# Output chains of the last head group one period later, and the queue engine's branch hint at the start of its stream

## The chip, the cores and the metric

The kernel runs on one core of one Trainium2 chip. The metric is the device time of one execution in microseconds (us). The profile's span is some 1.8 us shorter than that time (977.66 against 975.9 for the profiled run of the kernel before). Names of engines in the profile: PE is TensorE (matmuls), PEld its weight loads, ACT is ScalarE, DVE is VectorE, POOL is GpSimd, SP is SyncE, which issues nearly all DMA here.

## The reference

One sequence of 2048 rows and 1024 columns goes through two branches, and a gate per row mixes them:

```python
g = sigmoid((x * gate_w).sum(-1, keepdims=True))
a = A_ref(x, ...)            # a diagonal state-space layer: h = Lam_bar*h + Bu[t]; y = 2*Re(C h) + x*Dskip
b = B_ref(x, wqkv, wo)       # attention, 32 heads of 32 columns, then the output projection wo
return g * a + (1 - g) * b
```

What matters is the attention: 32 heads x 2048 x 2048 scores each need an exponential, and the output rows need the attention of all head groups before the projection `wo`.

## The kernel before

The program is planned in Python, in 512 periods. In period `p` PE computes the scores of one burst (4 heads, 256 queries, 256 keys), ScalarE takes two exponentials of 128x1024 from them, and PE multiplies the probabilities of burst `p - 2` with V. What PE has left in the period goes to blocks of four "dense" matmuls: projections, the state-space layer and, at the end, the output projection. Eight bursts make a unit (256 queries of one head group); there are 8 head groups of 8 units.

```python
def normalize(self, U):          # after the last burst of unit U: p % 8 == 1
    ...
    self.dma(lambda e: e.dma_start_transpose(self.OT[:, g, 256 * qb:256 * (qb + 1)]..., On[:, U % 2]...),
             [("On", U % 2)], [("OT", g, qb)] + x, "xp_o")

def d_out(self, qb, r, cb, k, js, kind):      # a chain: 8 matmuls = 2 periods; j is the head group
    for j in js:
        mms.append((1, lambda e, f, l, j=j: e.matmul(ps[:, 7, :], OT[:, j, ...], wo[j]..., start=f, stop=l),
                    [("OT", j, qb), wo[j][1]]))

# build(): when each output chain may start
seq = [(442, 6, r, cb, "part") for r, cb in rcb] + [(450, 7, r, cb, "part") for r, cb in rcb]
for qb in range(6):
    seq += [(458 + 8 * qb, qb, r, cb, "full") for r, cb in rcb]      # <- changed
seq += [(508, 6, r, cb, "rest") for r, cb in rcb]                    # one matmul each
```

The last matmul of a "full" chain (`j = 7`) reads the transpose that the last head group's unit has just started. After the last exponential comes a tail: the last probability-value matmuls, normalization, two PE transposes, four output matmuls, evacuation, two stores of 256 KB.

The fast path assumes that no softmax sum is out of range and checks this at the end. Every engine then reads a flag and branches over a slow fallback program. A hint in the instruction stream, placed by `MARK_AT`, is tied to that branch; what its place is worth is measured below (e2 and e6):

```python
MARK_AT = dict(pe=100, act=260, dve=260, pool=9999, sp=200)          # <- changed; counted back from the end
def stream(name, e):
    S.emit(name, e, sems, MARK_AT[name], lambda: loc.append(e.mark_branch_hint_location()))
    ...
    if name == "sp": S.final_waits(e, sems, False)                   # all DMAs but the last two
    e.wait_ge(sems[fast.flag_op.lane], fast.flag_op.tick)
    ... e.reg_load(r, flag[0:1, 0:1]); br = e.br_cmp(r, 0, on_true="done_" + name, ...); br.branch_hint(loc[0])
    ... # fallback program (cut)
    if name == "sp": S.final_waits(e, sems, True)                    # the last two stores
```

Of the kernel before, what the change touches and what calls it, by code (L numbers as in the profile page):

```python
# [937 lines left out]
class FastPath:  # L938
# [554 lines left out]
    def build(self):  # L1493
# [39 lines left out]
        rcb = [(r, cb) for r in range(2) for cb in range(2)]  # L1533
        seq = [(442, 6, r, cb, "part") for r, cb in rcb] + [(450, 7, r, cb, "part") for r, cb in rcb]
        for qb in range(6):
            seq += [(458 + 8 * qb, qb, r, cb, "full") for r, cb in rcb]
        seq += [(508, 6, r, cb, "rest") for r, cb in rcb]
        self.a_order = [4 * qb + 2 * r + cb for _, qb, r, cb, kind in seq if kind != "rest"]
        js = dict(full=range(8), part=range(7), rest=[7])
# [173 lines left out]
def bass_gated_mix__ssm_conv_s5__mha_block__prompt_kernel(  # L1713
    nc: bass.Bass,
    A_x: bass.AP,
    A_Lambda_re: bass.AP,
    A_Lambda_im: bass.AP,
    A_B_re: bass.AP,
    A_B_im: bass.AP,
    A_C_re: bass.AP,  # L1720
    A_C_im: bass.AP,
    A_log_dt: bass.AP,
    A_Dskip: bass.AP,
    B_x: bass.AP,
    B_wqkv: bass.AP,
    B_wo: bass.AP,
    gate_w: bass.AP,
    out: bass.AP,
):
    d = dict(A_x=A_x, A_Lambda_re=A_Lambda_re, A_Lambda_im=A_Lambda_im, A_B_re=A_B_re, A_B_im=A_B_im,  # L1730
             A_C_re=A_C_re, A_C_im=A_C_im, A_log_dt=A_log_dt, A_Dskip=A_Dskip, B_wqkv=B_wqkv, B_wo=B_wo,
             gate_w=gate_w, out=out)
    MARK_AT = dict(pe=100, act=260, dve=260, pool=9999, sp=200)
    with ExitStack() as es:
        S = Sched(n_dma_lanes=14)
        S2 = Sched(n_dma_lanes=12, pool_in_order=True, serial_xpose=True)
        sems = {l: es.enter_context(nc.semaphore("f_" + l)) for l in S.lanes()}
        sems2 = {l: es.enter_context(nc.semaphore("g_" + l)) for l in S2.lanes()}
        go = es.enter_context(nc.semaphore("go"))
        flag = es.enter_context(nc.sbuf_tensor("flag", [1, 1], I32))  # L1740
        with ExitStack() as fs:
            fast = FastPath(nc, S, fs, d, flag)
            fast.build()
            S.prepare()
        with ExitStack() as gs:
            c = gp_setup(nc, S2, gs, d)
            c.PA = GpPhaseA(c)
            c.items_done = 0
            gp_phase_c(c, gs)
            S2.barrier()  # L1750
            c.PA.finish(c.items_done)
            S2.prepare()
        block = es.enter_context(nc.Block())

        def stream(name, e):

            loc = []
            S.emit(name, e, sems, MARK_AT[name], lambda: loc.append(e.mark_branch_hint_location()))
            if not loc:
                loc.append(e.mark_branch_hint_location())  # L1760
            if name == "pool":
                for _ in range(272):
                    e.nop()
            if name == "sp":
                S.final_waits(e, sems, False)
            e.wait_ge(sems[fast.flag_op.lane], fast.flag_op.tick)
            with e.register("bad_" + name) as r:
                e.reg_load(r, flag[0:1, 0:1])
                br = e.br_cmp(r, 0, on_true="done_" + name, on_false="bad_" + name, comp_op="IS_EQ")
                br.branch_hint(loc[0])  # L1770
                with e.bass.body("bad_" + name):
                    if name == "sp":
                        S.final_waits(e, sems, True)
                        e.nop().then_inc(go, 1)
                    e.wait_ge(go, 1)
                    S2.emit(name, e, sems2)
                    if name == "sp":
                        S2.final_waits(e, sems2)
                    e.br("done_" + name)
                e.bass.switch_bb("done_" + name)  # L1780
            if name == "sp":
                S.final_waits(e, sems, True)

        @block.sync
        def _(e):
            stream("sp", e)

        @block.tensor
        def _(e):
            stream("pe", e)  # L1790

        @block.vector
        def _(e):
            stream("dve", e)

        @block.scalar
        def _(e):
            stream("act", e)

        @block.gpsimd  # L1800
        def _(e):
            stream("pool", e)
# [28 lines left out]
```

## Time and profile before

Runs of the kernel before: 979.44, 977.06, 979.46 and 977.79 us, median 978.62.

The first lines are from the page of the kernel before: span, busy time by engine, ACT's busy tenths in 40 slices, the granted clock of PE in tenths, and the costliest group (count, then busy us and mean ns, then idle time before it and its releaser).

```profile
span 975.9 us, 33479 instructions
...
PE 905.2 (93%) x15207; PEld 488.4 (50%) x15432; DVE 522.6 (54%) x1206; ACT 944.8 (97%) x1034; POOL 8.4 (1%) x46
...
ACT  4789999999999999999999999999999999999997
...
PEclk9999999999999999999999999999999999999998
...
L1454 ACT ACTIVATE f_pt<-f_ps 128x1024 bf16<-128x1024 f32 x1024 | 940.8, 1258 | 14.2 <-PE f_ps L1448 14.0
```

ScalarE is the limit: its exponentials fill the span. One exponential is 1258 ns in the table but they follow each other every 0.92 us, because the records of neighbours overlap. The idle column counts from the end of a record to the start of the next: at 886 us, after a record of 1.325, stands there 0.188 us.

The chain of waits of the kernel before, in order of time (start us, length us, what), around one place where ScalarE is not the limit:

```profile
880.57 0.74 PE f_ps L1401 x4
881.31 4.09 DMA f_OT<-f_On
885.40 0.05 issue
885.45 0.39 PE f_ps L1401
885.84 0.36 PE f_ps L1448 x8
886.22 3.82 ACT f_pt L1454 x4
```

The output matmul (L1401) waits for the DMA transpose, the scores (L1448) stand behind it in PE's order, and the exponential waits for the scores. The same pattern is at 940.32 us. The waits of the kernel before, 870 to 950 us (us in total, times, longest), show both occurrences, on PE and on the weight load:

```profile
PEld f_ps L1401 <- DMA f_OT<-f_On: 2.0, 2, 1.0
...
PE f_ps L1401 <- DMA f_OT<-f_On: 1.1, 2, 0.6
...
ACT f_pt L1454 <- PE f_ps L1448: 0.2, 1, 0.2
```

Busy time by engine in windows of 3.41 us near the end of the kernel before; the third number from the right is PE's granted clock:

```profile
core 0: us, PE busy (x) PEld busy (x) DVE busy (x) ACT busy (x) POOL busy (x), PEclk, DMA share, GB/s
952.69:956.11 3.42, 3.17 (x55) 1.55 (x53) 1.23 (x5) 3.42 (x4) 0.00 (x0) 1.00 0.00 0
956.11:959.52 3.41, 1.56 (x46) 0.93 (x43) 0.25 (x1) 3.41 (x5) 0.00 (x0) 1.00 0.32 101
959.52:962.94 3.42, 2.32 (x49) 1.32 (x50) 1.06 (x2) 3.42 (x5) 0.00 (x0) 0.50 0.00 0
962.94:966.35 3.41, 2.76 (x59) 1.58 (x54) 1.24 (x3) 3.41 (x5) 0.00 (x0) 0.50 0.21 77
966.35:969.76 3.41, 2.15 (x36) 1.32 (x33) 3.24 (x19) 1.54 (x4) 0.00 (x0) 1.00 0.22 79
```

After the last full output chain PE has little to do (46% busy from 956.11 us), and the clock falls to half for 6.83 us. It is back before the last exponential ends at 967.34 us. The tail from there to the end of the span is 8.60 us. The windows are aligned to the clock's changes in this trace.

### The profile page before, as it was taken

Reading aid. Unit: us, or ns where it says so; the run is one execution under the profiler, and the core shown is the slowest. Engines: PE = TensorE matmul, PEld = TensorE weight load, DVE = VectorE, ACT = ScalarE, POOL = GpSimd, SP = SyncE. Lnnn points to the kernel's source line nnn. Section 1 sums busy time; section 2 is a strip of 40 time slices with the busy share of each in tenths; the row PEclk is TensorE's granted clock in tenths of the full one; section 3 lists DMA queues with packets and bytes.
Section 4 is the critical chain, followed back from the end, with each engine's and each line's share of the span. In section 5 each row is a group of like instructions: output and inputs, shape, how many; then the busy total and the mean of one; then the engine's idle time right before and its main releaser. Section 6 shows DMA issues by size and latency. Waiting matters only on the chain.

```text
span 975.9 us, 33479 instructions
## 1 busy us (share of the span) xinstructions
PE 905.2 (93%) x15207; PEld 488.4 (50%) x15432; DVE 522.6 (54%) x1206; ACT 944.8 (97%) x1034; POOL 8.4 (1%) x46
## 2 busy tenths in 40 slices
PE   8889999999999999999999999999999999899995
PEld 5644554554444464444644644444554446444443
DVE  4897789877778854511257711177765112232223
ACT  4789999999999999999999999999999999999997
POOL 2000000000000000000000000000000000000000
PEclk9999999999999999999999999999999999999998
DMA  9992302311135202130022201142101213133311
GB/s 209 177 149 44 45 21 50 65 24 40 40 70 97 57 5 44 36 80 29 8 48 59 53 26 40 40 91 51 40 5 40 94 37 104 51 91 108 111 58 61
DMA packets 157011, 60.89 MB, mean 62 GB/s; under 512 B 145600, under 2 KB 145600, under 8 KB 156864
## 3 DMA queue, kind: packets, MB, share of 16 engines
q1 hardware_dynamic: 153664, 57.89, 26.6%
q8 instruction: 122, 2.00, 0.9%
q10 hardware_dynamic: 3200, 0.80, 0.4%
q14 instruction: 25, 0.20, 0.1%
HBM read 16.79 MB, written 12.58 MB: 30 GB/s over the span
## 4 chain that ended last, share of the span: by engine, by line
ACT 89%; DVE 5%; PE 4%; DMA 1%; issue 0%; DVEq 0%
ACT f_pt L1454 89%; DMA f_OT<-f_On 1%; DVE f_OT L1218 1%; DVE f_OT L1214 1%; PE f_ps L1313 1%; PE f_ps L1448 1%; PE f_ps L1069 1%; PE f_ps L1470 1%; DVE f_OT L1216 1%; DVE f_OT L1215 0%; PE f_ps L1401 0%; PE f_ps L1295 0%; DVE f_V L1319 0%; PE f_ps L1081 0%; PE f_ps L1344 0%
## 5 line engine op out<-in xcount | busy, mean ns | idle before, releaser
L1454 ACT ACTIVATE f_pt<-f_ps 128x1024 bf16<-128x1024 f32 x1024 | 940.8, 1258 | 14.2 <-PE f_ps L1448 14.0
L1470 PEld LDWEIGHTS f_ps<-f_V,f_pt 128*128 128x128 bf16 x8192 | 239.0, 96 | 109.9 <-issue 105.9
L1470 PE MATMUL f_ps<-f_V,f_pt 128*128 128x33 bf16 x8192 | 291.4, 178 | 0.5 <-DVE f_On L1484 0.5
L1448 PE MATMUL f_ps<-f_Q,f_K 32*128 32x256 bf16 x4096 | 204.7, 274 | 26.1 <-ACT f_pt L1454 7.7
L1448 PEld LDWEIGHTS f_ps<-f_Q,f_K 32*128 32x128 bf16 x4096 | 60.9, 92 | 242.4 <-ACT f_pt L1454 233.8
L1344 PE MATMUL f_ps<-f_xT,f_wb 128*128 128x512 bf16 x448 | 117.2, 377 | 13.8 <-DVE f_Q L1302 2.6
L1295 PE MATMUL f_ps<-f_xT,f_wb 128*128 128x512 bf16 x434 | 113.6, 379 | 9.2 <-issue 2.1
L1383 DVE TENSOR_SCALAR f_Ag<-f_ps,f_gcol 128x512 f32<-128x512 f32 x32 | 24.0, 751 | 139.8 <-PE f_ps L1368 139.8
L1244 DVE TENSOR_TENSOR_SCAN f_ht<-f_pf,f_init,f_ut 128x512 bf16<-128x512 f32 x64 | 80.4, 1273 | 0.0
L1368 PE MATMUL f_ps<-f_cT_im,f_hp 128*128 128x512 bf16 x192 | 72.6, 378 | 6.0 <-DVE f_Ag L1383 2.9
L1348 DVE CAST f_ub<-f_ps 128x512 bf16<-128x512 f32 x64 | 44.2, 691 | 51.9 <-PE f_ps L1344 51.8
L1313 PE MATMUL f_ps<-f_wb,f_xT 128*128 128x128 bf16 x1024 | 67.0, 219 | 0.0
L1401 PE MATMUL f_ps<-f_wb,f_OT 128*128 128x512 bf16 x218 | 58.5, 380 | 5.2 <-DVE f_xT L1407 1.7
L1344 PEld LDWEIGHTS f_ps<-f_xT,f_wb 128*128 128x128 bf16 x512 | 40.4, 96 | 36.2 <-issue 4.5
L1313 PEld LDWEIGHTS f_ps<-f_wb,f_xT 128*128 128x128 bf16 x1024 | 57.6, 97 | 0.4 <-issue 0.2
L1295 PEld LDWEIGHTS f_ps<-f_xT,f_wb 128*128 128x128 bf16 x496 | 39.3, 96 | 34.8 <-DMA f_xT<-in_A_x_dram 1.0
L1407 DVE SCALAR_TENSOR_TENSOR f_xT<-f_ps,f_gcol,f_hp 128x512 bf16<-128x512 f32 (+1 forms) x28 | 21.0, 751 | 64.3 <-PE f_ps L1401 64.3
L1368 PE MATMUL f_ps<-f_cT_re,f_hp 128*128 128x512 bf16 x144 | 54.4, 378 | 0.0
L1302 DVE CAST f_Q<-f_ps 128x512 bf16<-128x512 f32 x31 | 21.4, 691 | 51.3 <-PE f_ps L1295 51.3
L1235 DVE TENSOR_TENSOR f_tq<-f_ub,f_Et 128x512 bf16<-128x512 bf16 x128 | 46.3, 419 | 0.1
L1235 DVE TENSOR_TENSOR f_tq<-f_ht,f_Et 128x512 bf16<-128x512 bf16 x128 | 46.3, 417 | 0.0
L1319 DVE CAST f_V<-f_ps 128x512 bf16<-128x512 f32 x32 | 22.2, 693 | 42.0 <-PE f_ps L1313 42.0
(114 smaller groups left out, 428.4 us busy)
## 6 DMA issues: line engine op xcount, KB each, us to landing
ag_scratch<-f_Ag SPq DMA_DIRECT2D x32, 256.0 KB, 2.0
f_hp<-ag_scratch SPq DMA_DIRECT2D x32, 256.0 KB, 2.8
f_wb<-in_B_wqkv_dram SPq DMA_DIRECT2D x21, 256.0 KB, 4.4
out_dram<-f_xT SPq DMA_DIRECT2D x16, 256.0 KB, 2.3
f_wb<-in_B_wo_dram SPq DMA_DIRECT2D x1, 1024.0 KB
f_OT<-f_On SPq DMA_TRANSPOSE x63, 2.4
f_wb<-in_B_wqkv_dram ACTq DMA_DIRECT2D x3, 256.0 KB, 3.9
f_wb<-in_B_wo_dram SPq DMA_DIRECT2D x1, 768.0 KB, 4.6
```

The costliest lines, as they stand in the source:

```text
L1235: ops.append((c, lambda: dve(lambda e: e.tensor_tensor(o, a, b, op), r, w)))
L1244: ops.append((1.25, lambda ri=ri: dve(lambda e: e.tensor_tensor_scan(ht[:, ri, :], rr, ut[:, ri, :], self.init[:, ri, j:j + 1], ALU.mult, ...
L1295: mms.append((1, lambda e, f, l, a=a: e.matmul(ps[:, bank, :], w[:, g % 2, part, a, :], xT[:, a, 512 * ch:512 * (ch + 1)], start=f, stop=l ...
L1313: m = e.matmul(ps[:, bank, 128 * q:128 * (q + 1)], xT[:, a, 128 * kt:128 * (kt + 1)], w[:, g % 2, 2, a, :], start=(a == 0), stop=(a == 7))
L1344: mms.append((1, lambda e, f, l, a=a: e.matmul(ps[:, 7, :], bT[:, n % 2, ri, a, :], xT[:, a, 512 * ch:512 * (ch + 1)], start=f, stop=l), [ ...
L1348: self.dve(lambda e: e.tensor_copy(self.ub[:, n % 2, ri, :], ps[:, 7, :]), [("bank", 7)], [("ub", n % 2, ri)], "evac_u")
L1368: mms.append((1, lambda e, f, l, j=j, ri=ri: e.matmul(ps[:, 7, :], hp[:, ri, j, cols], cT[ri][:, j, 512 * cb:512 * (cb + 1)], start=f, sto ...
L1383: self.dve(lambda e: e.tensor_scalar(a, ps[:, 7, :], self.gcol[:, 0, tt:tt + 1], None, ALU.mult), [("bank", 7), "g0"], [at], "evac_c")
L1401: mms.append((1, lambda e, f, l, j=j: e.matmul(ps[:, 7, :], OT[:, j, 256 * qb + 128 * r:256 * qb + 128 * (r + 1)], wo[j][0][:, 512 * cb:51 ...
L1448: m = e.matmul(ps[:, 2 * sl[h // 2] + h % 2, 256 * kl:256 * (kl + 1)], K[32 * h:32 * h + 32, g % 2, 128 * kt:128 * (kt + 1)], Q[32 * h:32 ...
L1454: self.act(lambda e, s=s, p=p: e.activation(pt[:, p], ps[:, 2 * s:2 * s + 2, :], ACT.Exp, scale=SCALE), [("S", s)], [("pt", p)], "exp")
L1470: m = e.matmul(ps[:, 6, o:o + 33], pt[:, p, h2, 256 * kl + 128 * qt:256 * kl + 128 * (qt + 1)], V[:, g % 2, 2 * i + kl, h, :], start=(i == ...
```

## The change

The intent of the first part: a full chain starts one period (some 1.83 us) later, so that the transpose has arrived when its last matmul is due. The intent of the second: SyncE's hint should come early enough to have an effect, so it goes to the start of its stream.

```diff
-            seq += [(458 + 8 * qb, qb, r, cb, "full") for r, cb in rcb]
+            seq += [(459 + 8 * qb, qb, r, cb, "full") for r, cb in rcb]
@@
-    MARK_AT = dict(pe=100, act=260, dve=260, pool=9999, sp=200)
+    MARK_AT = dict(pe=100, act=260, dve=260, pool=9999, sp=900)
```

The order of the built instructions shows what it does on each engine: on PE the chains' blocks shift by one period, on SyncE the hint moves from behind the first transposed outputs to the front, and VectorE, ScalarE and GpSimd are unchanged.

## The prediction

> **What bounds the kernel now.** ScalarE. The page's first table gives ACT 944.8 of 975.9 us (97%), and the chain that ended last is 89% ACT, nearly all one line: 1024 exponentials of 128x1024, 1258 ns busy each but issued every 0.92 us (944 us for 1024). Idle before them is 14.2 us in all, in 15 pieces, most of it before 154 us. The stages by windows show ACT at 100% from 200 us to the tail except 0.19 us lost in 870 to 890 and 0.14 in 930 to 950. After the last exponential (967.35 us) follows a tail of 8.6 us.

> **First part: the output chains of full rows one period (1.83 us) later.** Nothing is added or removed: the same blocks of four matmuls on PE, the same DVE and ACT order. The last of the eight matmuls of a unit's first chain needs the transposed output of head group 7. In the timeline and the chain of waits this transpose is issued at 881.31 and 940.32 us and the matmul starts only 4.1 us later, after 0.55 us of PE waiting each. Because PE runs in order, the next scores come late, and ACT loses 0.19 and 0.14 us there. One period more is three times that wait, so both should go: about 0.33 us on the critical path.

> Side effect: the full chains end one period nearer the four "rest" chains, so one nearly matmul-free period (957 to 959 us) is left instead of two. The windows show PE's granted clock at 0.5 from 959.5 to 966.3 us, right after that lull. [...] It may now vanish or move. While ACT bounds, it is free; in the tail it is worth about 0.3 us either way.

> **Second part: SyncE's branch hint first in its stream instead of at 150.4 us.** It costs 62 ns, now before the first input load: start about 0.1 us later. [...] The trace agrees for GpSimd: from its branch at 970.88 to the next instruction 2.5 us, against 0.4 us on ACT. SyncE's branch (973.15) is followed by a wait that ends at 975.45, with the last store's last completion at 975.43 us: the landing ends last, a fetch stall would hide behind it. So the hint gives nothing, unless fetches delay the store (3.9 us against a median of 2.3): up to 0.5 us.

> **Sum.** -0.33 +0.1 -0.2 (hint, doubtful): -0.4 us, 0.04%, below the 2.4 us between the runs before (mean with the profiled one 978.4).

> Predicted: 978.2 us, range 975.8 to 980.6. Faster by over 2%: 0.01; within 2%: 0.98; slower: 0.01.

> **What would show it right.** No wait of the output matmuls for the output transpose after 870 us; ACT unbroken from 154 us to the tail; about 944.8 us of ACT. Half clock starting later or gone. SyncE's last wait still ending with the store's last completion.

> **What would make it wrong.** [...]SyncE stalls over 2 us past the landing; a delay of the first loads is larger than 62 ns; the tail falls in the half-clock stretch; a wider spread between runs.

The sum: it came to -0.33 + 0.1 - 0.2 = -0.43, given as -0.4 us. For GpSimd the 2.5 and 0.4 us are measured.

## The result, and the profile after

The changed kernel took 978.65, 979.8, 978.8 and 978.71 us, median 978.75, against 978.62 before. The ratio is 1.0006 with a 95% interval of 0.9988 to 1.0023: the same. Here and below a ratio is the mean time of one kernel's fast runs over that of the other's of the same rounds, so it is not quite the ratio of the quoted medians.

The page of the changed kernel:

```profile
span 976.9 us, 33704 instructions
...
PE 935.0 (96%) x15432; PEld 487.9 (50%) x15432; DVE 522.9 (54%) x1206; ACT 944.7 (97%) x1034; POOL 8.4 (1%) x46
```

PE's 935.0 against 905.2 us is no effect. The trace of the kernel before lacks 225 matmul records (15207 against 15432), and the program has the same matmuls. The chain of waits of the changed kernel, 930 to 950 us, is one unbroken piece:

```profile
929.30 21.08 ACT f_pt L1454 x23
```

These are all the waits that the same view lists for the changed kernel from 870 to 950 us. The lines of output matmuls waiting for the DMA are gone, and ScalarE waits for nothing:

```profile
DVE f_xT L1407 <- PE f_ps L1401: 61.8, 22, 5.0
PEld f_ps L1448 <- ACT f_pt L1454: 23.4, 44, 0.6
PEld f_ps L1470 <- issue: 9.3, 44, 0.2
DVE f_rc L1483 <- PE f_ps L1470: 1.1, 5, 0.2
```

So the first part did what it should. The windows near the end of the changed kernel, with the columns as before, show what happened beside it:

```profile
952.99:956.40 3.41, 3.33 (x56) 1.71 (x56) 1.39 (x4) 3.41 (x6) 0.00 (x0) 1.00 0.09 19
956.40:959.82 3.42, 2.41 (x51) 1.19 (x49) 0.75 (x1) 3.42 (x5) 0.00 (x0) 1.00 0.23 79
959.82:963.23 3.41, 2.00 (x50) 1.22 (x50) 1.50 (x2) 3.41 (x5) 0.00 (x0) 1.00 0.01 3
963.23:966.64 3.41, 2.81 (x45) 1.48 (x44) 1.55 (x4) 3.41 (x4) 0.00 (x0) 0.50 0.20 77
966.64:970.06 3.42, 2.62 (x23) 1.19 (x21) 2.60 (x18) 0.79 (x3) 0.00 (x0) 0.50 0.23 81
```

The half clock began later and stayed until the end. The last exponential now ended at 966.88 us, 0.46 us earlier than before, but the tail took 10.05 instead of 8.60 us.

The tool for everything that follows is a division of the span into pieces, from the start times of the 1024 exponentials, the issue of the last store and its last completion. "First" is the start of the first exponential; "70 to 870" the time between the starts of these two; "last store issued" counts from the end of the last exponential; "landed" from that issue to the last of its 16 completions. The tail is the sum of the last two and what remains to the end (0.5 to 1.0 us). All times are us, each from one profile.

| run | first | 0 to 70 | 70 to 870 | 870 to end of last | last store issued | landed | tail | span |
|---|---|---|---|---|---|---|---|---|
| before | 12.76 | 78.49 | 733.87 | 142.23 | +4.25 | 3.84 | 8.60 | 975.94 |
| as changed | 12.93 | 78.50 | 733.87 | 141.58 | +5.79 | 3.75 | 10.05 | 976.93 |
| e1 chains only | 14.09 | 78.49 | 733.88 | 141.58 | +5.79 | 3.68 | 9.97 | 978.01 |
| e2 hint only | 13.53 | 79.66 | 733.87 | 141.74 | +4.57 | 3.92 | 8.99 | 977.80 |
| e3 chains, PE filled | 13.09 | 79.64 | 733.87 | 141.58 | +3.91 | 3.92 | 8.34 | 976.52 |
| e4 before, PE filled | 13.41 | 78.48 | 733.88 | 141.72 | +3.91 | 3.86 | 8.28 | 975.77 |
| e5 filled, no branch | 13.15 | 80.76 | 733.88 | 141.58 | +3.91 | 2.11 | 6.50 | 975.88 |
| e6 hint late | 12.88 | 79.69 | 733.87 | 141.58 | +4.62 | 4.12 | 9.71 | 977.73 |
| e7 before, 506 filled | 13.02 | 79.66 | 733.87 | 141.72 | +4.58 | 4.12 | 9.20 | 977.48 |
| e8 filled, store waited for | 13.05 | 78.56 | 733.88 | 141.58 | +3.91 | 2.88 | 7.42 | 974.49 |
| a1 as changed, again | 13.30 | 78.49 | 733.87 | 141.58 | +4.25 | 3.96 | 8.72 | 975.96 |
| e9 before, both of e8 | 12.98 | 79.66 | 733.86 | 141.67 | +3.91 | 2.91 | 7.46 | 975.63 |
| e10 as e8, again | 12.61 | 78.48 | 733.87 | 141.58 | +3.91 | 2.75 | 7.33 | 973.87 |

Two things are to be seen at once. The 800 exponentials from 70 to 870 take the same time within 0.02 us in all thirteen profiles. And much of the spread between the profiles sits in the first two columns: the first exponential starts anywhere from 12.61 to 14.09 us, and 0 to 70 takes about 1.2 us or more longer in six of thirteen. Neither follows the change (e2 and e3 have the longer start, e1 and e4 have not). So the timed runs cannot show half a microsecond, and the pieces of the profile can.

The longer start goes with PE's clock. Five of the six (e2, e5, e6, e7, e9) have a half-clock window that begins between 33.10 and 33.91 us; none of the other eight profiles has one there. What takes longer in those five is exponentials 10 to 20: 15.5 to 15.8 us against 14.3. The two windows of e6, with the columns as before:

```profile
29.69:33.10 3.41, 1.75 (x36) 1.05 (x35) 3.23 (x13) 0.86 (x2) 0.00 (x0) 1.00 1.27 232
33.10:36.51 3.41, 3.41 (x44) 2.81 (x41) 1.59 (x5) 1.30 (x3) 0.00 (x0) 0.50 1.25 164
```

The sixth, e3, loses its time between exponentials 0 and 10 (16.1 us against 14.9 to 15.0) without such a window, and e5 loses some there too; the reason was not looked for.

### The profile page after: what moved, and what is told of

It reads as the page before. It is cut to its first block, busy times and chain, and to the rows that moved or that the text cites. A ratio compares the mean times of both kernels' runs of the same rounds, so it can differ in the third digit from the quotient of the medians.

```text
span 976.9 us, 33704 instructions
## 1 busy us (share of the span) xinstructions
PE 935.0 (96%) x15432; PEld 487.9 (50%) x15432; DVE 522.9 (54%) x1206; ACT 944.7 (97%) x1034; POOL 8.4 (1%) x46
## 4 chain that ended last, share of the span: by engine, by line
ACT 90%; DVE 5%; PE 3%; SPq 1%; DMA 0%; issue 0%
ACT f_pt L1454 90%; DVE f_OT L1218 1%; PE f_ps L1313 1%; DVE f_OT L1214 1%; PE f_ps L1470 1%; DVE f_OT L1216 1%; SPq L1020 0%; PE f_ps L1295 0%; PE f_ps L1448 0%; DVE f_OT L1215 0%; DMA f_xT<-in_A_x_dram 0%; PE f_ps L1344 0%; DVE f_V L1319 0%; DVE f_Et L1220 0%; DVE f_K L1302 0%
## 5 line engine op out<-in xcount | busy, mean ns | idle before, releaser
L1344 PE MATMUL f_ps<-f_xT,f_wb 128*128 128x512 bf16 x512 | 131.0, 377 | 2.4 <-DVE f_ub L1348 0.9
L1295 PE MATMUL f_ps<-f_xT,f_wb 128*128 128x512 bf16 x496 | 128.2, 382 | 2.3 <-DVE f_V L1319 1.3
L1368 PE MATMUL f_ps<-f_cT_re,f_hp 128*128 128x512 bf16 x192 | 72.8, 379 | 0.3
L1401 PE MATMUL f_ps<-f_wb,f_OT 128*128 128x512 bf16 x252 | 65.9, 380 | 0.0
```

The costliest lines, as they stand in the source:

```text
L1295: mms.append((1, lambda e, f, l, a=a: e.matmul(ps[:, bank, :], w[:, g % 2, part, a, :], xT[:, a, 512 * ch:512 * (ch + 1)], start=f, stop=l ...
L1344: mms.append((1, lambda e, f, l, a=a: e.matmul(ps[:, 7, :], bT[:, n % 2, ri, a, :], xT[:, a, 512 * ch:512 * (ch + 1)], start=f, stop=l), [ ...
L1368: mms.append((1, lambda e, f, l, j=j, ri=ri: e.matmul(ps[:, 7, :], hp[:, ri, j, cols], cT[ri][:, j, 512 * cb:512 * (cb + 1)], start=f, sto ...
```

## The experiments

The theory: moving the chains removes the two pauses of ScalarE, and PE's half clock, shifted into the tail, gives the gain back; the hint does nothing beyond its own issue time. The rivals are told with each run. Each kernel was right against the reference. From e3 on, where the text does not say otherwise, SyncE's hint is where it was before (`sp=200`). The timed runs had five rounds each, beside nine runs of the kernel before on the same chip in each set. Medians of before: 978.95 us (e1 to e4), 978.21 (e5 to e8) and 977.58 (a1, e9, e10).

### e1_chains_only: the chains moved, the hint as before

```diff
-                seq += [(458 + 8 * qb, ...
+                seq += [(459 + 8 * qb, ...
```

> Only the chains are moved; the hint stays where it was. Theory (two opposite effects of the move): ScalarE loses none of the 0.59 and 0.55 us it lost at 886 and 945 us before, so exponential number 1000 starts about 1.1 us earlier counted from the first exponential; after the last exponential the tail takes 8.6 us if the clock is full there and about 10 us if it is halved, so the time is 978.6 within 1 us and the same as the kernel with both parts, less about 0.17 us at the start. Rival (the hint is what lost the time): the tail is 8.6 us at whatever clock and the time is about 1.1 us under that of before.

Measured: 979.75 us median, ratio 1.0005 (0.9992 to 1.0019). The profile repeats the changed kernel piece by piece: 141.58 us from exponential 870 to the end, last store issued at +5.79 us, half clock from 3.57 us before the end of the last exponential to the end of the span. Exponential 1000 started 931.54 us after the first, against 932.43 before: 0.89 us, not the 1.1 expected. The median lies 0.15 us outside the 1 us allowed, with a start that is 1.33 us late. The rival, that the hint lost the time, falls: without it the tail is as long.

### e2_hint_only: the hint moved, the chains as before

```diff
-    MARK_AT = dict(pe=100, act=260, dve=260, pool=9999, sp=200)
+    MARK_AT = dict(pe=100, act=260, dve=260, pool=9999, sp=900)
```

> Only the hint is moved. Theory: the start is 0.1 to 0.2 us later, the stretch of exponentials as before with both losses of 0.55 to 0.6 us, SyncE's last wait still ends within 0.1 us of the last completion of the last store, and the time is that of before plus 0.1 to 0.2 us, not to be told from zero. Rival (the hint delays SyncE's branch or the last store): about 1 us slower than before with the tail 1 us or more longer at the same clock.

Measured: 979.58 us, ratio 1.0001 (0.9987 to 1.0015). SyncE's last wait ended 0.02 us after the last completion (977.31 and 977.29 us), as before. The pauses of ScalarE are there but smaller than expected: two gaps of 0.41 and 0.24 us above the usual spacing. The direct cost of the hint is visible at SyncE's first DMA issue. These are the first issues in the timelines of the kernel before and of this one:

```profile
0.82 3.12 SPq L1020 DMA_TRANSPOSE f_xT<-in_A_x_dram  x2
```

```profile
0.91 3.22 SPq L1020 DMA_TRANSPOSE f_xT<-in_A_x_dram  x2
```

It is 0.93 in the changed kernel and 0.80 in e1. So 0.1 us, far below the 1.5 us by which the first exponential wanders.

### e3_chains_warm: the chains moved, the quiet periods of PE filled

```diff
+    def keep_warm(self, n):      # results are never read
+        for i in range(n):
+            self.S.op("pe", lambda e, i=i: e.matmul(self.ps[:, 7, :], self.ident[:], self.K[:, 1, 512*(i%4):512*(i%4)+512], start=True, stop=True),
+                      reads=["ident", ("K", 1, i % 4)], writes=[("bank", 7)], name="warm")
@@ build(), in each period
+            if 505 < p < 511 and cur is None and (not outs or outs[0][0] > p or len(outs[0][1].pieces) == 1):
+                self.keep_warm(4 if not outs or outs[0][0] > p else 3)
@@ tail()
         self.pv(NBURST - 1)
+        self.keep_warm(3)
```

> The chains moved, the hint as before, and matmuls whose result nobody reads fill PE in the quiet periods (4 in period 507, 3 in each of 508 to 510, 3 after the last probability-value block). Theory (the half clock in the tail eats the gain): the granted clock is 1.0 throughout the tail, the score matmuls there take 0.40 us and not 0.61, the tail after the last exponential is 8.3 to 8.8 us and the time about 977.2, some 1.3 us under the kernel as changed and under before by about 1.1. Rival (the tail is long for other reasons, such as the store's landing): the tail stays at 9.5 to 10 us.

Measured: 978.65 us, ratio 0.9997 (0.9983 to 1.0011), so the time expected (977.2) was not reached; the profiled run (978.25) is 1.15 us longer between exponentials 0 and 70. The pieces are as the theory said. The windows near the end of this kernel:

```profile
956.40:959.82 3.42, 3.35 (x56) 1.62 (x56) 0.75 (x1) 3.42 (x5) 0.00 (x0) 1.00 0.14 31
959.82:963.23 3.41, 3.33 (x56) 1.71 (x56) 0.75 (x1) 3.41 (x6) 0.00 (x0) 1.00 0.19 70
963.23:966.64 3.41, 3.40 (x57) 1.64 (x56) 1.50 (x2) 3.41 (x5) 0.00 (x0) 1.00 0.20 77
```

PE is busy for 98% and more, the clock stays at 1.00, the last store is issued at +3.91 us instead of +5.79, and the tail is 8.34 us. The half clock alone is worth 1.88 us of the changed kernel's tail. The rival falls.

### e4_before_warm: the kernel before, the quiet periods filled

The edit is that of e3 without the moved chains; four filling matmuls go into each of the periods 506 and 507.

> The kernel before, chains and hint unmoved, with the same filling matmuls (4 in each of periods 506 and 507). Theory: full clock in the tail in every run, so the slower of the runs of before disappear (about 979.4) and all lie near 977.5 to 978.3; the two losses of about 0.57 us on ScalarE stay, so it is about 1.0 us slower than the chains moved with filling. Rival: no change against before.

Measured: 978.38 us (977.6 to 980.16), ratio 1.0000 (0.9986 to 1.0014). The clock is full throughout the tail and the store is issued at +3.91 us, as in e3. But the slow runs did not disappear, although the filling is the same in each; so the tail's clock, seen in the one profiled run alone, is unlikely to be what makes them slow. The two gaps of ScalarE were 0.25 and 0.40 us here, and from exponential 870 to the end the kernel is only 0.14 us behind the moved chains, not 1.0. The single spacings in the trace show why. In this stage exponentials follow each other after 0.913 and 0.921 us in turn. After a pause 14 to 25 of them come after 0.9035 us and win back much of what was lost. Why they can, the runs do not show.

### e5_warm_nobranch: e3 without branch and fallback

```diff
-            S.emit(name, e, sems, MARK_AT[name], lambda: loc.append(e.mark_branch_hint_location()))
+            S.emit(name, e, sems)
-            ... (flag wait, load, branch, fallback program, 272 nops of GpSimd)
```

The landing of the last store was the open question: 3.7 to 3.9 us in each profile, against a median of 2.3 for the 16 output stores of the kernel before. This kernel leaves out a needed safety branch on purpose; its results are right for these inputs.

> Chains moved, PE filled, and the branch with the fallback code behind it taken out (the flag is still computed, nothing reads it; the results are right for these inputs). Theory (the fetches of the engines' next instructions after their branches hold up the last store's packets): no instruction fetch between the last two stores and the end, the last store lands 2.0 to 2.6 us after its issue instead of 3.7 to 3.9, and the tail after the last exponential is about 6.8 to 7.2 us instead of 8.34. Rival (two stores of 256 KB back to back take that long by themselves): the landing stays at 3.7 us or more and only the tail's last few tenths change.

Measured: 976.17 us, ratio 0.9981 (0.9968 to 0.9995), the only kernel whose interval excludes 1. The profiled run was one of its slow ones (977.6; 80.76 us between exponentials 0 and 70), so its span is no shorter than before. Its tail, 6.50 us, is below the 6.8 to 7.2 expected. The DMA view of the last six microseconds, of the kernel before and then of this one (the q14 and q8 lines are instruction fetches; the last line has KB and median us to landing of the last two stores):

```profile
q1 hardware_dynamic: 291, 0.53, 26.6%
q14 instruction: 5, 0.04, 2.2%
q8 instruction: 1, 0.02, 1.0%
...
out_dram<-f_xT SPq DMA_DIRECT2D x2, 256.0 KB, 2.7
```

```profile
q1 hardware_dynamic: 361, 0.64, 28.9%
...
out_dram<-f_xT SPq DMA_DIRECT2D x2, 256.0 KB, 2.0
```

The changed kernel, in the same view, is like the kernel before:

```profile
q1 hardware_dynamic: 288, 0.52, 26.2%
q14 instruction: 5, 0.04, 2.7%
q8 instruction: 1, 0.02, 1.1%
...
out_dram<-f_xT SPq DMA_DIRECT2D x2, 256.0 KB, 4.0
```

Without branches there is no fetch in the window, and all 16 completions of the last store come between 1.94 and 2.11 us after its issue. With branches most of the 16 are done 2.1 us after the issue and a few stragglers come up to 2.0 us later: in the kernel before 12 by 973.70 us, then 974.41, 975.06, 975.07 and 975.43. The fetches that follow the taken branches hold those up; a fetch packet of 8 KB took 0.31 to 0.83 us and PE's 16 KB about 1.0 us, against 0.084 us for most of the store's 2 KB packets. The rival falls. This run takes out more than the fetches; e8 below holds some of them back and leaves the rest as it is.

### e6_hint_late: the changed kernel with SyncE's hint right before the branch

```diff
-    MARK_AT = dict(..., sp=900)
+    MARK_AT = dict(..., sp=0)
```

> The kernel as changed, but SyncE's hint right before its branch, as late as it can be. Theory (the hint's place does not matter because the wait for the store ends later than any fetch): SyncE's last wait still ends within 0.1 us of the last completion, the landing takes 3.6 to 4.1 us, the tail is 9.9 to 10.2 us with half clock, time within 0.3 us of the kernel as changed apart from the start. Rival (a hint far ahead saves a fetch): SyncE's last wait ends 0.5 us or more after the last completion, or there is one fetch more after SyncE's branch, and the tail is over 10.4 us.

Measured: 978.77 us, ratio 1.0004 (0.9991 to 1.0018). Here the theory was wrong and the rival all but right. The last completion was at 976.75 us but SyncE's wait ended at 977.24, 0.49 us later (the rival said 0.5 or more) and 2.96 us after SyncE's branch. There was also one fetch more at the end than in the other kernels with a branch, but at 977.80 us, after that wait, so it is not what held the wait up. In this one profile, then, a hint given 1.26 us before the branch (at 973.02 us) did not spare SyncE a stall of half a microsecond past the landing, while hints 150 us and 0.8 us into the kernel are equally good: 0.02 us between last completion and end of wait in every one of those runs. The tail, 9.71 us, is below the rival's 10.4 because the half clock fell differently: 6.49 us before the end of the last exponential to 0.33 us after it.

### e7_before_fill506: the kernel before with PE filled in period 506 alone

```diff
+            if p == 506:
+                self.keep_warm(4)
```

PE's load then has the outline of the changed kernel's, with everything else unmoved.

> The kernel before, chains and hint unmoved, with four filling matmuls in period 506 alone: PE's load is then as in the kernel as changed (full until the end of 506, one quiet period, then one matmul per period), but DVE, the stores and the waits are as before. Theory (the half clock comes later because the quiet stretch begins a period later): the clock halves 2.5 to 5.5 us before the last exponential ends, not 6.6 to 7.8, and does not come back before the end; the tail is 9.5 to 10.1 us, while the losses of 0.25 to 0.6 us at 886 and 945 us stay. Rival (the moved chains' own work on DVE and the stores lengthens the tail): the tail stays at 8.6 to 9.0 us.

Measured: 979.21 us, ratio 1.0009 (0.9995 to 1.0022). The tail of 9.20 us fits neither range. The clock was halved from 6.57 us before to 0.26 us after the end of the last exponential and the store issued at +4.58 us: within 0.1 us what e6 shows, which has the same PE load by way of moved chains. So the moved chains need no cost of their own on VectorE or in the stores to explain e6. More does not follow: e2, with the chains and PE's load of the kernel before, shows the same pattern (halved from 6.60 us before to 0.23 us after, store at +4.57 us). The load of the changed kernel can give another pattern than the +5.79 us of its first profile, and two different loads can give the same one.

### e8_warm_waitstore: e3, and three engines wait for the last store but one

```diff
             e.wait_ge(sems[fast.flag_op.lane], fast.flag_op.tick)
+            if name in ("pe", "act", "dve"):
+                o = [o for o in S.all_ops if o.is_dma][-2]
+                e.wait_ge(sems[o.lane], 16 * S.final_count[o.lane])
```

> Chains moved, PE filled, and PE, ScalarE and VectorE wait for the landing of the last store but one before they read the flag and branch, so that their fetches start after most of the last store is through. Theory (fetches hold the last store up): the last store lands about 2.5 to 3.2 us after its issue and the tail is 7.3 to 8.0 us, about 0.5 us under the kernel with filling alone; VectorE's and PE's own branch end before the last landing. Rival (the store is slow by itself, or GpSimd's and SyncE's fetches are the ones that matter): the landing stays at 3.7 to 3.9 us and the tail at 8.3 us or over.

Measured: 976.56 us, ratio 0.9987 (0.9974 to 1.0001). The landing fell to 2.88 us and the tail to 7.42 us. PE's fetch of 16 KB, at 973.49 us in e3 in the midst of the store, came at 974.86 us, 1.0 us after the last completion. GpSimd's fetch (at 971.26 us, 0.69 us long) still falls into the store, and 0.8 us over the 2.11 of e5 stay; all other fetches begin at 973.65 us or later, when the store's data packets are through. VectorE's branch ended before the last landing, as expected, PE's 0.27 us after it.

### a1_after_again: the changed kernel once more

> The kernel as changed, once more, with five timed rounds, to be read beside the next two on the same chip. Theory [...]: 870 to 1000 of the exponentials take 119.2 us as in the first profile; the last store is issued either 5.8 us after the last exponential (clock halved some 3.6 us before it and to the end) or 4.6 us after it (halved some 6.5 us before it, back just after it), and lands 3.6 to 4.1 us later; time within 0.15% of the kernel before. Rival (moving the chains always puts the half clock over the whole tail): 5.8 us again, and the time 0.5 us or more over that of before.

Measured: 977.79 us, ratio 1.0003 (0.9989 to 1.0016). Its windows, with the columns as before:

```profile
956.28:959.70 3.42, 2.42 (x49) 1.23 (x48) 0.75 (x1) 3.42 (x5) 0.00 (x0) 1.00 0.30 96
959.70:963.11 3.41, 1.76 (x46) 0.96 (x44) 1.50 (x2) 3.41 (x5) 0.00 (x0) 1.00 0.02 5
963.11:966.52 3.41, 2.53 (x58) 1.77 (x60) 1.08 (x2) 3.41 (x5) 0.00 (x0) 0.50 0.20 77
966.52:969.93 3.41, 2.20 (x27) 1.15 (x25) 3.01 (x19) 1.44 (x4) 0.00 (x0) 1.00 0.23 82
```

A third pattern, which neither expectation named: halved for one window only, back 0.71 us before the last exponential ends, store issued at +4.25 us. The rival, that the moved chains always put the half clock over the whole tail, falls. The span is 975.96 us, that of the kernel before within 0.02.

### e9_before_warm_waitstore and e10_warm_waitstore_again

e9 is e8 with the chains unmoved; e10 is e8 again.

> Chains unmoved, PE filled in the quiet periods, and PE, ScalarE and VectorE waiting for the last store but one before they branch. Theory (the parts add up): last store issued 3.9 us after the last exponential and landed in 2.5 to 3.1 us, as with the chains moved; exponentials 870 to 1000 take 119.5 to 120.1 us instead of 119.2, so 0.3 to 0.9 us over the next kernel apart from the start. Rival (the gain of the moved chains is made up elsewhere): the time from the first to the last exponential is the same as with the chains moved.

> The combination that the runs so far point to (chains moved, PE filled, the three engines waiting for the last store but one), once more beside the kernel as changed on the same chip. Theory: exponentials 870 to 1000 in 119.2 us, last store issued 3.9 us after the last exponential, landed in 2.5 to 3.1 us, tail 7.2 to 7.7 us; 976.6 us, about 1.5 to 2.3 us (0.15 to 0.25%) under both the kernel before and the kernel as changed. Rival (its lead was the luck of one set of runs): within 0.5 us of both.

Measured, e9: 977.06 us, ratio 0.9991 (0.9977 to 1.0004); e10: 977.15 us, ratio 0.9994 (0.9981 to 1.0008). In the profiles the parts add up: both issue the last store at +3.91 us and land it in 2.91 and 2.75 us. Unmoved chains cost e9 0.09 us from exponential 870 to the end, still less than the 0.3 expected, because its two gaps were 0.34 and 0.13 us. e10's span of 973.87 us is the shortest of all, with a tail 1.27 us shorter than before. But its median leads by only 0.43 us over before and 0.64 over a1, not the 1.5 expected, and its interval contains 1. That the combination is faster is shown piece by piece in the profiles; the timed runs lean the same way in both sets and do not prove it.

## Why the prediction was right or wrong

The measured 978.75 us lies in the range of 975.8 to 980.6, 0.55 us from the predicted 978.2, and the kernels are the same, as said. Point by point:

- **ScalarE is the bound.** Right: 733.87 us from exponential 70 to 870 in every kernel, whatever was changed around it.
- **The two waits for the output transpose go.** Right, in all eight profiles with moved chains: 141.58 us from exponential 870 to the end each time. The size, 0.33 us, came from a wrong reading: the idle column showed 0.19 and 0.14 us, but spacings show pauses of 0.59 and 0.55 us beyond the usual spacing, since overlapping records hide most of a pause. The net gain was 0.65 us in that profile, because the exponentials after a pause come closer, and 0.09 to 0.16 us in the four other profiles with unmoved chains. That the estimate landed inside 0.09 to 0.65 was luck: it knew of neither effect.
- **The half clock in the tail is worth about 0.3 us either way.** The author's estimate, given without its working, and the mis-sized term. Against a full clock (+3.91 us to the last store) it measured 0.34 us where it ended before the last exponential, 0.66 to 0.71 where it ended just after it, and 1.88 us where it lasted to the end. In the changed kernel's first profile the tail grew by 1.45 us, which swallowed the whole gain and made the sum +0.99 us instead of -0.4; in its second profile, tail and span were as before. The changes near the end lie one or two times 3.41 us apart, and from the span's start the clock was halved at 959.52 us before, at 963.23 and 963.11 in the two profiles of the changed kernel and at 961.52 in e6. In those two profiles it stayed halved to the end once and for 3.41 us once. Which pattern a run gets was therefore a lottery here, and moving the quiet stretch one period later moved it closer to the tail. That this makes a long tail more likely is not shown: of the profiles without filling, the clock stayed halved to the end in two of the four with moved chains and in neither of the two with the chains and load of before.
- **The hint costs about 0.1 us at the start.** Right: first DMA issue at 0.93 and 0.91 us with it, 0.82 and 0.80 without.
- **The hint gives nothing, and a fetch stall would hide behind the landing.** The first half is right: with the hint 150 us into the kernel SyncE's wait ends 0.02 us after the last completion, as it does with the hint at 0.8 us. The second is wrong by half a microsecond: in e6 the late hint shows as 0.49 us after the last completion. Long stretches after a branch were measured on SyncE in e6 (2.96 us from branch to the end of its next wait) and on GpSimd (2.6 us from branch to next instruction in the kernel before, where ScalarE took 0.5). That the engine waits there for a fetch was the author's estimate and is not shown.
- **Fetches delay the last store by up to 0.5 us.** The direction was right and the size too small: against e5's 2.11 us it is 1.6 to 2.0 us. The fetches there come after the engines' branches (the first branch at 970.88 us, the first of the six fetches at 971.90 in the kernel before), and no place of SyncE's hint removed them: six with the hint at 150 us and at 0.8 us, one more in e6.

That the median came out where it was forecast rests on small terms of both signs below a noise of 2 us. The forecast "the same" was safe; its -0.4 us was not shown.

## What to carry to other kernels

When an off-path engine stops holding up the bound one, ask where its quiet time has moved: here PE's lull moved 1.83 us closer to the tail, where PE's clock counts for once (1.88 us of the changed kernel's tail). The end of a kernel is a stage of its own, and a last transfer can be held up by fetches of instructions that nobody waits for; make the branches wait rather than the data (here the last store then landed after 2.75 to 2.91 us instead of 3.7 to 4.1; the timed runs do not prove a gain). When run-to-run noise exceeds the effect, divide the profile at events that every version has, and compare pieces; read pauses of an engine with overlapping records from start-to-start spacing and not from the idle column.
